# A three-stage kernel on one core: the low parts of expert weights, all made by VectorE instead of half by GpSimd

## The chip, the core and the metric

The kernel runs on one core of a Trainium2 chip. The metric is the device time of one execution in microseconds (us). Times before and after are medians of several runs; the profile is one further execution with the hardware profiler on. The engines are named as in the profile's rows: PE (TensorE matmuls), PEld (TensorE weight loads), DVE (VectorE), ACT (ScalarE), POOL (GpSimd) and SP (SyncE, which here only issues DMAs).

## What is computed

Three layers follow one another: a gated linear attention, a dense layer with squared ReLU, and a mixture of experts in which every token goes to one of eight experts. Everything is float32.

```python
def _moe2_ref(x, w_gate, w1, w2):        # x: 3072 x 384, w1: 8 x 384 x 1024, w2: 8 x 1024 x 384
    logits = x @ w_gate
    expert_idx = np.argmax(logits, axis=1)
    ...
    for e in range(E):
        mask = expert_idx == e
        ...
        h = np.maximum(x[mask] @ w1[e], 0.0)
        out[mask] = gate_w[mask, None] * (h @ w2[e])

def reference(**kwargs):
    attn_out = _attn_ref(**attn_kwargs)               # gated linear attention, 4 x 8 heads, 768 x 48
    ...
    x = _moe_ref(x=x, **moe_kwargs)                   # h = relu(x @ w_in); h * h @ w_out, 384 -> 2048 -> 384
    return _moe2_ref(x=x, **moe2_kwargs)
```

## The kernel before, in words

**Products in three parts.** A float32 matrix product is done as three matmuls in the type fp32r. Each operand is split into a high part, its copy rounded to fp32r, and a low part, the operand minus its high part. The product is then low times high, plus high times low, plus high times high. Every expert weight therefore needs a split before PE can use it: ACT copies the raw tile to `w_hi` (L612), and a tensor-tensor subtraction on DVE or POOL makes `w_lo` (L613). Both lines are in `split_part`.

**Stages.** Up to about 480 us, attention groups alternate with the dense layer, whose eight groups of 384 tokens are interleaved with the next group's attention. From about 480 to 545 us the last dense group runs alone; in it, `ph` (L404) is the first product, `gg`, `gh`, `gl` (L410 to L417) its activation and split, `po` (L434) the second product. From about 546 us to the end the experts run.

**Expert steps.** The experts are worked off in 16 steps that are set out in `KINDS`: 12 steps of kind D (256 token slots of one expert) and 4 of kind S (128 slots). A step gathers its tokens by an indirect DMA (`xg`, L620, POOL's queue), and has eight slots `i`. In slot `i`, `step_h` makes one 128-wide part of the hidden layer, `ph` (nine matmuls, L981; in an S step six or so plain float32 matmuls on the raw weights, L969), then `hh` (ACT, L985) and `hl` (DVE, L986). `step_out` multiplies `hh` and `hl` with the second weight matrix into `qo` (D) or `qs` (S, L1001). It runs two slots later in a D step and three later in an S step. At a step's end ACT scales the result (`o`, L1013), and POOL's queue scatters it to `out` (L1014).

**Weights.** An expert's weights are loaded in eight pieces, `rawt[j]` for j = 0 to 7, 384 KB each (L634, SP's queue). In the listings of instructions below these eight buffers are called raw_5241 (j = 0) to raw_5248 (j = 7). Pieces 0 to 3 hold the first matrix, 4 to 7 the second. Piece `j` of step `s` is split into the set `wst_[s % 2][j]`, w_hi_154 for even steps and w_hi_155 for odd ones, each with its own `w_lo`. An S step splits only pieces 4 to 7. `split_plan` fixes in which slot each piece is split. As soon as a piece is split, the next step's load into the same `rawt[j]` is issued on SP's queue, which is worked off in order and holds these loads one behind the other.

**Who sets the order.** PE and ACT run in the order in which the program is written. The order on DVE, POOL and SP in the expert steps comes from a scheduler that simulates the program. Each engine then runs its own list strictly in order.

**The line in question.** `split_w` (called from `run_steps` for steps 1 to 15) gives the subtraction to POOL for the pieces in `lo_pool(s)`: j = 1, 3, 5, 7, or 3, 5, 7 when the step before is of kind S. Step 0's pieces are split in the last dense group by a direct call of `split_part`, always on DVE.

Of the kernel before, what the change touches and what calls it, by code (L numbers as in the profile page):

```python
# [19 lines left out]
B, H, S, D = 4, 8, 768, 48  # L20
# [15 lines left out]
KINDS = "DD" + "DDDSDDSDDSDDDS" + "SSS"  # L36
# [20 lines left out]
def gla_moe_moe_kernel(ctx: ExitStack, tc: tile.TileContext, qk, ft, vt, w_in, w_out, w_gate, w_gateT, w_e, q, k, v, f_logit, out, dbg=None):  # L57
    nc = tc.nc
# [548 lines left out]
    rawt, xg = [], []  # L607
    wst_ = []
    ids_t, esi_t, reg_t, x_s, out_t = {}, {}, {}, {}, {}

    def split_part(hi, lo, src, eng=nc.vector):
        nc.scalar.activation(out=hi, in_=src, func=AF.Copy)  # L612
        eng.tensor_tensor(out=lo, in0=src, in1=hi.bitcast(F32), op=ALU.subtract)  # L613
# [331 lines left out]
    early["split"], early["ready"] = [], False  # L945
    SPLITS = split_plan()


    def lo_pool(s):
        return (3, 5, 7) if KINDS[s - 1] == "S" else (1, 3, 5, 7)  # L950

    def split_w(s, j):
        if s == NEARLY - 1:
            early["split"].append(j)
        split_part(*wst_[s % 2][j], rawt[j], nc.gpsimd if j in lo_pool(s) else nc.vector)

    def wslice(s, which, a, n):
        j, o = divmod(a, WP)
# [85 lines left out]
    def run_steps(s0, s1, hook=None, pend=(), flush=True):  # L1044
        pend = list(pend)
        for s in range(s0, s1):
            if s == NALWAYS - 1:
                tc.mark_branch_hint_location("rest")
            for i in range(8):
                pend.append((s, i, *step_h(s, i)))  # L1050
                while len(pend) > (2 if KINDS[s] == "D" else 3):
                    step_out(*pend.pop(0))
                if i == 0 and s + 2 != NEARLY:
                    load_x(s + 2)
                if KINDS[s] == "S" and i % 2:
                    load_w(s + 1, i // 2)
                for t, j in SPLITS.get((s, i), ()):
                    split_w(t, j)
                    if t + 1 != NEARLY or early["ready"]:
                        load_w(t + 1, j)  # L1060
                if hook:
                    hook(s, i)
                if i == (5 if KINDS[s] == "D" else 3):
                    prep_next(s + 1)
        if flush:
            for p in pend:
                step_out(*p)
        return pend
# [302 lines left out]
```

## Time and profile before

| | before |
|---|---|
| median of 3 runs | 824.01 us (823.91 to 825.7) |
| the profiled execution | 823.52 us |
| its span, first to last instruction | 821.7 us |
| mean granted TensorE clock | 0.989 of full speed |
| PE busy | 785.1 us, 96% |
| DVE busy | 548.8 us, 67% |
| ACT busy | 414.2 us, 50% |
| POOL busy | 159.9 us, 19% |

The span is what the profile's times count from; about 1.8 us of the execution lie outside it. Busy time is the time in which an engine worked on an instruction, including any time in which that instruction itself was held up. A granted clock of 1.00 is 2.4 GHz, and 0.50 is 1.2 GHz.

### The profile page before, as it was taken

To read this page: it belongs to the slowest core of one execution; us is meant where nothing else is said; L and a number is where in the kernel's file an instruction comes from. 1 tells how busy PE (TensorE), PEld (TensorE's weight loads), DVE (VectorE), ACT (ScalarE), POOL (GpSimd) and SP (SyncE) were. 2 spreads that over 40 slices of the span, in tenths; PEclk is the share of its full clock that TensorE was granted. 3 is DMA by queue.
4 is the path that set the end of the run, shared out by engine and by line. 5 is a ranking of instruction groups with operands and counts; after the bars stand their busy time and mean duration, and the time that the engine had idled before them with its cause. 6 is when DMAs were issued, how large, how long until landed. Compare 5 with 4: busy or idle time off the path is not lost.

```text
span 821.7 us, 15286 instructions
## 1 busy us (share of the span) xinstructions
PE 785.1 (96%) x5681; PEld 729.6 (89%) x5681; DVE 548.8 (67%) x1266; ACT 414.2 (50%) x830; POOL 159.9 (19%) x158
## 2 busy tenths in 40 slices
PE   5799999999999999999999999989999999999995
PEld 4566679999999999999999999989999899898995
DVE  7979779768768767767767654568566545656641
ACT  2233466455455454454455454753465465555651
POOL 2000000000000000000000011212656466555551
PEclk9899999999999999999999999999999999999998
DMA  9886321112131121130120015314666766758640
GB/s 266 238 266 179 126 47 52 45 53 56 43 88 38 49 63 45 46 98 25 45 69 1 2 43 205 107 59 168 238 210 223 255 218 206 268 177 277 203 143 29
DMA packets 40563, 102.09 MB, mean 124 GB/s; under 512 B 5630, under 2 KB 9442, under 8 KB 40352
## 3 DMA queue, kind: packets, MB, share of 16 engines
q1 hardware_dynamic: 36896, 91.57, 36.3%
q0 software_dynamic: 3584, 9.46, 3.1%
q8 instruction: 47, 0.77, 0.4%
q14 instruction: 36, 0.29, 0.1%
HBM read 91.31 MB, written 10.24 MB: 124 GB/s over the span
## 4 chain that ended last, share of the span: by engine, by line
PE 76%; DVE 8%; issue 6%; DMA 5%; ACT 4%; POOL 1%; SPq 0%; POOLq 0%; DVEq 0%; ACTq 0%
PE po L434 22%; PE ph L404 20%; PE qo L1001 8%; PE ph L981 8%; DVE w_lo L613 4%; PE ph L394 4%; DMA raw<-w_e 3%; PE pa L263 3%; PE py L319 3%; ACT w_hi L612 2%; PE ph L969 1%; PE py L299 1%; PE pu L309 1%; PE qs L1001 1%; DMA xT<-xT 1%
## 5 line engine op out<-in xcount | busy, mean ns | idle before, releaser
L410 ACT ACTIVATE gg<-ph 128x384 f32<-128x384 f32 x128 | 62.7, 490 | 180.8 <-PE ph L404 128.3
L417 DVE TENSOR_TENSOR gl<-gg,gh 128x384 fp32r<-128x384 f32 x112 | 63.4, 566 | 84.4 <-ACT gh L415 83.2
L404 PE MATMUL ph<-xh,w_lo 128*128 128x384 f32 x336 | 118.7, 353 | 0.9 <-ACT gg L410 0.9
L434 PE MATMUL po<-w_hi,gl 128*128 128x384 f32 x336 | 113.8, 339 | 2.2 <-DVE gl L417 2.2
L404 PE MATMUL ph<-xl,w_hi 128*128 128x384 f32 x336 | 114.4, 340 | 0.6 <-DVE xl L162 0.6
L404 PE MATMUL ph<-xh,w_hi 128*128 128x384 f32 x336 | 113.9, 339 | 0.0
L434 PE MATMUL po<-w_hi,gh 128*128 128x384 f32 x336 | 113.7, 338 | 0.0
L434 PE MATMUL po<-w_lo,gh 128*128 128x384 f32 x336 | 113.2, 337 | 0.0
L613 DVE TENSOR_TENSOR w_lo<-raw,w_hi 128x768 fp32r<-128x768 f32 x63 | 94.4, 1500 | 24.0 <-ACT w_hi L612 18.2
L613 POOL TENSOR_TENSOR w_lo<-raw,w_hi 128x768 fp32r<-128x768 f32 x49 | 91.1, 1875 | 82.8 <-ACT w_hi L612 80.4
L612 ACT ACTIVATE w_hi<-raw 128x768 fp32r<-128x768 f32 x112 | 93.8, 839 | 19.8 <-DMA raw<-w_e 19.6
L986 DVE SCALAR_TENSOR_TENSOR hl<-ph,hh 128x256 fp32r<-128x256 f32 (+1 forms) x128 | 48.8, 387 | 78.8 <-ACT hh L985 76.3
L985 ACT ACTIVATE hh<-ph 128x256 fp32r<-128x256 f32 (+1 forms) x128 | 45.2, 356 | 97.5 <-PE ph L981 72.4
L708 POOL MEMSET xg<- 128x385 f32 x4 | 1.5, 422 | 466.9 <-DVE gl L417 466.9
L981 PE MATMUL ph<-xh,w_lo 128*128 128x256 f32 x288 | 82.8, 288 | 5.9 <-DVE w_lo L613 5.9
L458 DVE SCALAR_TENSOR_TENSOR junk<-rows,wgb 128x384 f32<-128x384 f32 x144 | 80.0, 555 | 3.3
L981 PE MATMUL ph<-xl,w_hi 128*128 128x256 f32 x288 | 81.4, 283 | 0.0
L981 PE MATMUL ph<-xh,w_hi 128*128 128x256 f32 x288 | 81.1, 282 | 0.0
L411 ACT ACTIVATE gg<-gg 128x384 f32<-128x384 f32 x128 | 67.2, 525 | 4.0
L404 PEld LDWEIGHTS ph<-xh,w_lo 128*128 128x128 f32 x336 | 63.0, 187 | 6.9 <-issue 3.1
L1001 PE MATMUL qo<-w_hi,hl 128*128 128x384 f32 x192 | 66.4, 346 | 1.7 <-DVE hl L986 1.3
L434 PEld LDWEIGHTS po<-w_hi,gl 128*128 128x128 f32 x336 | 63.3, 189 | 2.8 <-DVE gl L417 2.5
(236 smaller groups left out, 1653.9 us busy)
## 6 DMA issues: line engine op xcount, KB each, us to landing
raw<-w_e SPq DMA_DIRECT2D x128, 384.0 KB
qk<-qk SPq DMA_DIRECT2D x46, 192.0 KB
v<-vt SPq DMA_DIRECT2D x24, 256.0 KB
stg<-w_in SPq DMA_DIRECT2D x8, 768.0 KB
stg<-w_out SPq DMA_DIRECT2D x8, 768.0 KB
f<-ft SPq DMA_DIRECT2D x24, 226.2 KB
xs<-rows SPq DMA_DIRECT2D x8, 577.5 KB
wgb<-w_gateT SPq DMA_DIRECT2D x1, 1536.0 KB
```

The costliest lines, as they stand in the source:

```text
L404: nc.tensor.matmul(ph, lhsT=w[:, sl], rhs=x[:, k, :], start=(n == 0), stop=(n == 8))
L410: nc.scalar.activation(out=gg, in_=ph, func=AF.Relu)
L411: nc.scalar.activation(out=gg, in_=gg, func=AF.Square)
L417: nc.vector.tensor_tensor(out=gl, in0=gg, in1=gh.bitcast(F32), op=ALU.subtract)
L434: nc.tensor.matmul(po[m], lhsT=a[:, sl], rhs=w[:, ws], start=(i == 0 and n == 0), stop=(i == NF - 1 and n == len(terms) - 1),)
L458: nc.vector.scalar_tensor_tensor(out=junk, in0=rows[:, m, 0:DM], scalar=1.0, in1=wgb[0][:, e, :], op0=ALU.mult, op1=ALU.mult, accum_out=lg ...
L612: nc.scalar.activation(out=hi, in_=src, func=AF.Copy)
L613: eng.tensor_tensor(out=lo, in0=src, in1=hi.bitcast(F32), op=ALU.subtract)
L981: nc.tensor.matmul(ph, lhsT=wslice(s, w, (i * 3 + k) * 128, 128), rhs=x[:, k, :], start=(n == 0), stop=(n == 8))
L985: nc.scalar.activation(out=hh, in_=ph, func=AF.Relu)
L986: nc.vector.scalar_tensor_tensor(out=hl, in0=ph, scalar=0.0, in1=hh.bitcast(F32), op0=ALU.max, op1=ALU.subtract)
L1001: nc.tensor.matmul(out_t[s][m], lhsT=x[:, sl], rhs=wslice(s, w, 3 * F2 + i * DM, DM), start=(i == 0 and n == 0), stop=(i == 7 and n == 2),)
```

## The change

`lo_pool` goes, and `split_w` no longer passes an engine, so every subtraction goes to `split_part`'s default, VectorE:

```diff
-    def lo_pool(s):
-        return (3, 5, 7) if KINDS[s - 1] == "S" else (1, 3, 5, 7)
-
     def split_w(s, j):
         if s == NEARLY - 1:
             early["split"].append(j)
-        split_part(*wst_[s % 2][j], rawt[j], nc.gpsimd if j in lo_pool(s) else nc.vector)
+        split_part(*wst_[s % 2][j], rawt[j])
```

The program on PE and on ACT stays the same instruction for instruction. DVE's list grows by 49 subtractions, which POOL's list loses, and SP keeps its loads in the same order, with some reads of a register value moved between the first loads of step 2. Line numbers behind the edit shift by 4, so L986 is L982 afterwards.

**Where an S step ends and a D step begins.** The listing below is DVE's, from the fifth slot of the first S step (step 5) on. Before:

```order
L613 TENSOR_TENSOR w_lo<-raw_5247,w_hi_154 128x768
L986 SCALAR_TENSOR_TENSOR hl<-ph_7281,hh 128x128
L643 TENSOR_TENSOR xl_7299<-px,xh_7298 128x3x128 x2
L986 SCALAR_TENSOR_TENSOR hl<-ph_7314,hh 128x128
L986 SCALAR_TENSOR_TENSOR hl<-ph_7325,hh 128x128
L613 TENSOR_TENSOR w_lo<-raw_5241,w_hi_154 128x768
L986 SCALAR_TENSOR_TENSOR hl<-ph_7340,hh 128x128
L986 SCALAR_TENSOR_TENSOR hl<-ph_7351,hh 128x128
L613 TENSOR_TENSOR w_lo<-raw_5242,w_hi_154 128x768
```

The same place now:

```order
L613 TENSOR_TENSOR w_lo<-raw_5247,w_hi_154 128x768
L982 SCALAR_TENSOR_TENSOR hl<-ph_7281,hh 128x128
L613 TENSOR_TENSOR w_lo<-raw_5248,w_hi_154 128x768
L643 TENSOR_TENSOR xl_7299<-px,xh_7298 128x3x128 x2
L982 SCALAR_TENSOR_TENSOR hl<-ph_7314,hh 128x128
L982 SCALAR_TENSOR_TENSOR hl<-ph_7325,hh 128x128
L613 TENSOR_TENSOR w_lo<-raw_5241,w_hi_154 128x768
L982 SCALAR_TENSOR_TENSOR hl<-ph_7340,hh 128x128
L982 SCALAR_TENSOR_TENSOR hl<-ph_7351,hh 128x128
L613 TENSOR_TENSOR w_lo<-raw_5242,w_hi_154 128x768
```

Piece 7's subtraction (raw_5248) came from POOL's list. It now stands ahead of the split of the gathered tokens (`xl`) and four rows ahead of piece 0 of the D step (raw_5241).

**Within a D step.** DVE's list in step 2, where the pieces of step 3 are split; `hl` is one row per slot. Before:

```order
L986 SCALAR_TENSOR_TENSOR hl<-ph_6606,hh 128x256
L613 TENSOR_TENSOR w_lo<-raw_5241,w_hi_155 128x768
L986 SCALAR_TENSOR_TENSOR hl<-ph_6640,hh 128x256
L986 SCALAR_TENSOR_TENSOR hl<-ph_6663,hh 128x256
L613 TENSOR_TENSOR w_lo<-raw_5245,w_hi_155 128x768
L986 SCALAR_TENSOR_TENSOR hl<-ph_6686,hh 128x256
L613 TENSOR_TENSOR w_lo<-raw_5243,w_hi_155 128x768
L643 TENSOR_TENSOR xl_6711<-px,xh_6710 128x3x128 x2
L986 SCALAR_TENSOR_TENSOR hl<-ph_6726,hh 128x256
L986 SCALAR_TENSOR_TENSOR hl<-ph_6749,hh 128x256
```

Now:

```order
L982 SCALAR_TENSOR_TENSOR hl<-ph_6606,hh 128x256
L613 TENSOR_TENSOR w_lo<-raw_5241,w_hi_155 128x768
L982 SCALAR_TENSOR_TENSOR hl<-ph_6640,hh 128x256
L613 TENSOR_TENSOR w_lo<-raw_5242,w_hi_155 128x768
L982 SCALAR_TENSOR_TENSOR hl<-ph_6663,hh 128x256
L613 TENSOR_TENSOR w_lo<-raw_5245,w_hi_155 128x768
L982 SCALAR_TENSOR_TENSOR hl<-ph_6686,hh 128x256
L613 TENSOR_TENSOR w_lo<-raw_5243,w_hi_155 128x768
L643 TENSOR_TENSOR xl_6711<-px,xh_6710 128x3x128 x2
L982 SCALAR_TENSOR_TENSOR hl<-ph_6726,hh 128x256
L613 TENSOR_TENSOR w_lo<-raw_5246,w_hi_155 128x768
L982 SCALAR_TENSOR_TENSOR hl<-ph_6749,hh 128x256
```

Slots that had no subtraction between two `hl` now have one; no two stand next to each other here.

**At the end of the last dense group.** DVE's list where pieces of step 0 (w_hi_154) and step 1 (w_hi_155) are split between the `gl` of that group. Before:

```order
L417 TENSOR_TENSOR gl<-gg,gh 128x384 x2
L613 TENSOR_TENSOR w_lo<-raw_5243,w_hi_154 128x768
L417 TENSOR_TENSOR gl<-gg,gh 128x384
L613 TENSOR_TENSOR w_lo<-raw_5244,w_hi_154 128x768
L613 TENSOR_TENSOR w_lo<-raw_5243,w_hi_155 128x768
```

Now:

```order
L417 TENSOR_TENSOR gl<-gg,gh 128x384
L613 TENSOR_TENSOR w_lo<-raw_5242,w_hi_155 128x768
L417 TENSOR_TENSOR gl<-gg,gh 128x384
L613 TENSOR_TENSOR w_lo<-raw_5243,w_hi_154 128x768
L417 TENSOR_TENSOR gl<-gg,gh 128x384
L613 TENSOR_TENSOR w_lo<-raw_5244,w_hi_154 128x768
L613 TENSOR_TENSOR w_lo<-raw_5243,w_hi_155 128x768
```

Piece 1 of step 1 (raw_5242 with w_hi_155) is made by DVE between two `gl`; everything else keeps its order.

## Rows read from the trace of the kernel before

**Rows 1.** Waits of PE, 500 to 822 us: total us, times, longest.

```profile
PE ph L981 <- DVE w_lo L613: 5.9, 3, 2.0
PE po L434 <- DVE gl L417: 2.2, 1, 2.2
PE qo L1001 <- DVE hl L986: 1.3, 7, 0.2
```

**Rows 2.** Groups by line and shape: busy us, mean ns | idle before.

```profile
L613 DVE TENSOR_TENSOR w_lo<-raw,w_hi 128x768 fp32r<-128x768 f32 x63 | 94.4, 1500 | 24.0 <-ACT w_hi L612 18.2 <-issue 5.4 <-DMA raw<-w_e 0.3
...
L613 POOL TENSOR_TENSOR w_lo<-raw,w_hi 128x768 fp32r<-128x768 f32 x49 | 91.1, 1875 | 82.8 <-ACT w_hi L612 80.4 <-DMA raw<-w_e 2.1
L417 DVE TENSOR_TENSOR gl<-gg,gh 128x384 fp32r<-128x384 f32 x112 | 63.4, 566 | 84.4 <-ACT gh L415 83.2
...
L986 DVE SCALAR_TENSOR_TENSOR hl<-ph,hh 128x256 fp32r<-128x256 f32 x96 | 39.9, 421 | 61.7 <-ACT hh L985 60.5 <-issue 0.5
...
L162 DVE TENSOR_TENSOR w_lo<-w_raw,w_hi 128x768 fp32r<-128x768 f32 x16 | 15.3, 956 | 4.4 <-ACT w_hi L161 4.3
```

**Rows 3.** Timeline at the first change from S to D: start, us, engine.

```profile
649.46 1.82 POOL L613 TENSOR_TENSOR w_lo<-raw,w_hi 128x768 fp32r<-128x768 f32 x1
649.48 2.62 DVE L613 TENSOR_TENSOR w_lo<-raw,w_hi 128x768 fp32r<-128x768 f32 x1 [0.45 <-issue]
...
652.15 0.39 PE L981 MATMUL ph<-xh,w_lo 128*128 128x256 f32 x1 [1.97 <-DVE w_lo L613]
652.20 0.85 ACT L612 ACTIVATE w_hi<-raw 128x768 fp32r<-128x768 f32 x1 [1.83 <-DMA raw<-w_e]
```

**Rows 4.** Timeline within a D step.

```profile
592.39 4.79 DVE L613 TENSOR_TENSOR w_lo<-raw,w_hi 128x768 fp32r<-128x768 f32 x1 [0.31 <-ACT w_hi L612]
592.69 3.67 POOL L613 TENSOR_TENSOR w_lo<-raw,w_hi 128x768 fp32r<-128x768 f32 x2
597.11 0.74 DVE L986 SCALAR_TENSOR_TENSOR hl<-ph,hh 128x256 fp32r<-128x256 f32 x2
```

**Rows 5.** Chain of waits, 596 to 605 us: start, us, what.

```profile
597.57 1.32 PE qo L1001 x6
...
600.59 1.06 PE qo L1001 x6
```

**Rows 6.** Chain of waits, 649 to 660 us.

```profile
652.15 1.51 PE ph L981 x9
...
655.59 1.54 PE ph L981 x9
```

**Rows 7.** Chain of waits, 697 to 706 us: the second change from S to D.

```profile
701.35 1.32 PE ph L981 x9
...
703.72 1.07 PE ph L981 x9
...
705.31 0.71 PE ph L981 x6
```

**Rows 8.** Windows: busy us of PE, PEld, DVE, ACT, POOL; PEclk; DMA share; GB/s.

```profile
544.00:546.00 2.00, 2.00 (x8) 2.00 (x7) 1.72 (x4) 0.57 (x2) 0.00 (x0) 0.50 0.31 54
...
654.00:656.00 2.00, 2.00 (x8) 2.00 (x8) 1.47 (x3) 0.82 (x2) 0.00 (x0) 0.50 1.06 349
```

**Rows 9.** Timeline of DVE in the last dense group.

```profile
521.27 1.35 DVE L417 TENSOR_TENSOR gl<-gg,gh 128x384 fp32r<-128x384 f32 x1 [3.09 <-ACT gh L415]
```

**Rows 10.** Timeline at the end of the last dense group.

```profile
540.28 0.85 ACT L612 ACTIVATE w_hi<-raw 128x768 fp32r<-128x768 f32 x1 [2.04 <-DMA raw<-w_e]
...
542.65 0.79 DVE L417 TENSOR_TENSOR gl<-gg,gh 128x384 fp32r<-128x384 f32 x1 [3.34 <-ACT gh L415]
...
543.49 0.44 PE L434 MATMUL po<-w_hi,gl 128*128 128x384 f32 x1 [2.15 <-DVE gl L417]
```

**Rows 11.** Timeline at 666 us: a subtraction beside a DMA issue of POOL.

```profile
666.23 0.96 DVE L613 TENSOR_TENSOR w_lo<-raw,w_hi 128x768 fp32r<-128x768 f32 x1 [0.31 <-ACT w_hi L612]
666.70 1.40 POOL L620 DMA_INDIRECT xg<-xs,ids  x1 [0.67 <-PE px L641]
```

## The prediction

> **What bounds the kernel now.** I read the profile from PE outward. PE is busy 96% of the span, so the first view is what PE waits for in the stretch that the edit touches. From 500 us to the end three waits make nearly all of PE's idle time, and DVE ends each of them [rows 1]: 5.9 us in three pieces until a `w_lo`, 2.2 us in one piece until a `gl`, 1.3 us in seven pieces until an `hl`. The question is then why DVE is late, although it is busy only 67% of the span.
>
> The groups by line answer it. A subtraction of 128x768 on DVE takes 0.956 us in the dense stage, where POOL has nothing of the kind; the same shape at L613, with POOL at work on its own 49, takes 1.50 us on average over 63 [rows 2]. POOL's take 1.875 us each. Then I looked at the places in order of time. At the first change from an S step to a D step, POOL starts a subtraction at 649.46 and ends at 651.28; DVE's, started at 649.48, takes 2.62 us and ends at 652.10, 0.82 us after POOL's; PE, which had run dry 1.97 us before, starts at 652.15 [rows 3]. Within a D step DVE's subtraction of 592.39 lasts 4.79 us, to 597.18, again 0.82 us behind the end of POOL's two back to back at 596.36 [rows 4]. So while POOL runs such an operation, DVE's does not advance, and the reader can see the price of POOL's help: it comes out of DVE's time, and out of the time of what stands behind it in DVE's list.
>
> **The change part by part.** POOL loses 49 operations of 1.875 us. DVE gets 49 of 0.96 us, 47 us of work; it gets back what the overlap cost it, 63 x (1.50 - 0.96) = 34 us, so its busy time should rise by only about 13 us, to some 562 us. What matters is where.
>
> *Changes from S to D, three of them.* Piece 0 of the D step would take 0.96 instead of 2.62 us, end at 650.44, and let PE start at 650.49, 0.31 us after it runs dry: 1.66 us each, 5.0 us for the three waits of 1.97. The added piece 7 now stands four rows ahead of piece 0. DVE was idle for 0.45 us before piece 0 [rows 3] and elsewhere in the S step; if the addition found no other room, piece 0 would start 0.96 - 0.45 = 0.51 us late, 1.5 us over the three. I take nothing for it, since it stands ahead of two `hl` whose inputs come later, and keep 1.5 for the range.
>
> *D steps.* Seven waits for `hl` give 1.3 us [rows 1], 0.19 each. After one, the next six matmuls take 1.32 us instead of 1.06 [rows 5], so a wait costs 0.45 and the seven 3.2 us. An `hl` behind a subtraction of 0.96 us instead of 4.79 comes 3.8 us earlier, and PE waited only 0.19, so the waits go wholly, with over 3 us of slack. The price: other slots now have a subtraction in front of their `hl`. Each can delay its `hl` by at most 0.96 us, under the 3 us, so I cost it at nothing. The cover is the two slots between `hl` and its use; without it each of some 50 slots would cost up to 0.96.
>
> *The clock.* After the first S-to-D wait the clock fell to 0.50 of 2.4 GHz, that is 1.2 GHz [rows 8]. For nine matmuls, six and nine more PE needed 4.98 us, 652.15 to 657.13 [rows 6]; behind the second such wait the same took 3.44 us, 701.35 to 704.79 [rows 7]. With a wait of 0.31 us I expect no fall: 1.5 us. The lower bound is nothing, if the fall has another cause.
>
> *The end of the last dense group.* PE waits 2.15 us for a `gl` that took 0.79 instead of about 0.56 us (the mean of all is 0.566 [rows 2]), because POOL was at work: 0.23 us. That `gl` was late since ACT stood 2.04 us for a load [rows 10], and loads are issued when DVE has done the piece before. A `gl` of 1.35 us at 521.27 [rows 9] held up this chain by 0.79 us. DVE now makes the added piece there itself, just before that `gl`; I keep 0.5 of the 0.79. Together 0.7 us, between 0 and 1.0. Behind this wait too the clock is 0.50 [rows 8]; whether a wait of 1.4 us instead of 2.15 still brings that is open. I leave it as it is; if it goes, another 1.5 us or so goes with it.
>
> *Queues.* SP's loads keep their order, and wait for DVE where they waited for POOL; a piece is done 0.9 us sooner or more, so no load is issued later. The register reads moved between step 2's first loads let its second load start sooner and none later than before; nothing in [rows 1] waits for these loads, so I take nothing for it. POOL's gathers and scatters no longer queue behind subtractions. A DMA issue beside a DVE subtraction takes 1.40 us, and the subtraction stays 0.96 [rows 11]; the issues have POOL almost to themselves now.
>
> Sum: 5.0 + 3.2 + 1.5 + 0.7 = 10.4 us. The profiled execution took 823.52 us, so 813.1; the median of the runs is 0.5 us above it, so **813.6 us**.
>
> A rule that speaks against one term: the Trainium skill, in "SBUF — State Buffer", section "Who interferes with whom", says that DVE operations with two SBUF inputs and GpSimd operations that read SBUF exclude each other, and that whoever issues first holds the ports for the whole instruction. The trace agrees that one blocks the other, but not on the order: DVE's operation began 0.30 us before POOL's and still ended after both [rows 4]. Taken strictly, the rule would not explain the 4.79 us, and the 3.2 us of the D steps would stay; it is the third rival below.
>
> **The rivals.**
>
> *DVE becomes the bound (slower).* One mechanism: subtractions stay long without POOL's, because DMA issues on POOL hold DVE as its subtractions did. A D step lasts 8 x (1.06 + 1.07) = 17.0 us [rows 5, 7], and DVE must then do 8 subtractions and 8 `hl` of 0.42 [rows 2]. At 0.96 that is 11.0 us; it decides at (17.0 / 8) - 0.42 = 1.7 us per subtraction. At POOL's own 1.875 us it is 18.4 us, 1.4 us too much in each of some ten D steps: 14 us more with no wait saved, about 838 us. For it speaks the mean of 1.50; against it the 0.96 us beside a DMA issue [rows 11] and the 0.956 without POOL. Chance 0.03.
>
> The skill's "Perfetto Trace Analysis", section "Optimizing Scalar/DVE Operations", advises to offload when DVE is saturated, and warns that between DVE and GpSimd it might not help, as they share a port. The trace shows 11.0 of 17.0 us, not saturated.
>
> *The wait moves to the load of piece 1.* At the first S-to-D change ACT starts piece 1 at 652.20, having waited 1.83 us for its load [rows 3]; split, it is ready near 654.1. PE needs it with the third group of nine in the D step, 705.31 - 701.35 = 3.96 us after its start [rows 7], so at 654.45 when it starts at 650.49: 0.35 us of slack. Loads that were held behind POOL now start sooner and share the DMA engines. One load of 384 KB at 349 GB/s [rows 8] is 1.1 us; if that much is put in front of piece 1, PE waits 0.75 us, three times: 2.3 us, so 815.9. Against it: piece 1's load is issued before the freed ones. Chance 0.13.
>
> *Only the S-to-D waits shrink*, the `hl` waits having another cause: 816.8. Chance 0.05, as each ends 0.82 us behind POOL in both pictures.
>
> *The clock.* If the fall at 652 us stays in spite of the short wait, 815.1: 0.07. If the one at 544 us goes too, 812.1: 0.22.
>
> *No change* within 0.2% (1.6 us): the waits would have to come back in equal size elsewhere, as for loads: 0.04.
>
> **How the numbers follow.** The forecast has 0.46. Its own case and those of the clock and the load run from 812.1 to 815.9; adding 1.5 for a late piece 0 to the forecast gives 815.1, and up to 0.3 more at the dense group's end and the residual 0.31 three times give 810.9 at the best. With 816.8 included, the range is **811.0 to 817.0**, which leaves out the last case and the slower one, and some of the tails. A measurement of this kernel can tell about 0.2%. Faster by more than that: 0.46 + 0.13 + 0.05 + 0.07 + 0.22 = 0.93, same 0.04, slower 0.03.
>
> **What would show it.** In the profile after, L613 on DVE should be 112 operations of about 0.96 us, and POOL should have none. The three waits of PE for `w_lo` should be about 0.3 us each, those for `hl` gone, the wait for `gl` about 1.4 us, and PEclk 1.00 near 650 us. I am wrong if L613 stays well above 0.96 us, if PE waits in the middle of D steps for `hl`, or if the wait for piece 0 turns into one for piece 1 with a DMA as its releaser.

## The result, and the profile after

The changed kernel took 816.38 us (median of 5 runs, 815.77 to 819.04), the kernel before 825.2 us (5 runs, 823.91 to 827.79) in the same comparison: ratio 0.9897, 95% interval 0.9873 to 0.9922. The gain is 8.8 us where 10.4 were forecast; 816.38 lies inside the range 811.0 to 817.0. The profiled execution took 815.93 us with a span of 814.2, 7.6 us below the 823.52 of before.

Waits of PE from 500 to 822 us in the changed kernel (us in total, times, longest):

```profile
PE po L434 <- DVE gl L417: 1.5, 1, 1.5
PE qo L997 <- ACT o L1009: 1.0, 1, 1.0
PE ph L977 <- DVE w_lo L613: 0.6, 2, 0.4
PE pl L484 <- ACT xt L476: 0.4, 1, 0.4
PE pi L672 <- DVE sel L668: 0.4, 1, 0.4
PE pl L484 <- DVE xt L478: 0.3, 1, 0.3
```

The 5.9 us for `w_lo` of [rows 1] have become 0.6 and the waits for `hl` are gone; those for `o` and `xt` are new, the one for `sel` was there before. Groups by line and shape (busy us, mean ns | idle before):

```profile
L613 DVE TENSOR_TENSOR w_lo<-raw,w_hi 128x768 fp32r<-128x768 f32 x112 | 106.9, 956 | 47.8 <-ACT w_hi L612 44.0 <-issue 2.7 <-DMA raw<-w_e 1.0
L417 DVE TENSOR_TENSOR gl<-gg,gh 128x384 fp32r<-128x384 f32 x112 | 62.0, 554 | 78.4 <-ACT gh L415 74.4 <-ACT gg L411 2.6
```

All 112 subtractions take 0.956 us, against 1.50 in [rows 2]. The first change from S to D, timelines of DVE, ACT and PE:

```profile
648.98 0.96 DVE L613 TENSOR_TENSOR w_lo<-raw,w_hi 128x768 fp32r<-128x768 f32 x1
...
652.84 0.85 ACT L612 ACTIVATE w_hi<-raw 128x768 fp32r<-128x768 f32 x1 [2.25 <-DMA raw<-w_e]
...
654.74 0.39 PE L977 MATMUL ph<-xh,w_lo 128*128 128x256 f32 x1 [0.23 <-DVE w_lo L613]
```

Piece 0 takes 0.96 us instead of 2.62 [rows 3], and PE doesn't wait for it at all. But ACT waits 2.25 us for the load of piece 1, and PE then 0.23 us for that piece. Windows of the changed kernel (columns as in [rows 8]):

```profile
552.00:554.00 2.00, 2.00 (x11) 2.00 (x11) 1.69 (x10) 0.22 (x1) 0.00 (x0) 0.51 0.03 8
...
654.00:656.00 2.00, 1.77 (x13) 1.45 (x13) 2.00 (x4) 1.76 (x4) 0.29 (x1) 1.00 1.01 398
```

The clock stays at 1.00 at 654 us, where it was 0.50. The fall of 544 us has moved to 552 us, behind two new short waits for `xt`. They have a cause on ACT (timeline):

```profile
548.61 0.84 ACT L612 ACTIVATE w_hi<-raw 128x768 fp32r<-128x768 f32 x1 [2.02 <-DMA raw<-w_e]
549.36 0.37 ACT L981 ACTIVATE hh<-ph 128x256 fp32r<-128x256 f32 x1
549.62 0.48 ACT L476 ACTIVATE xt<-pt 128x384 f32<-128x384 f32 x1
```

ACT stands 2.02 us for a load of step 1's piece 6, and `hh` and `xt` queue behind it. In the kernel before it stood 0.69 us there:

```profile
547.63 0.84 ACT L612 ACTIVATE w_hi<-raw 128x768 fp32r<-128x768 f32 x1 [0.69 <-DMA raw<-w_e]
```

**Three stretches.** All kernels of this case have one common mark where the work of the tables ends: the two small products `pi` (L672), each of which waits for `sel` on DVE. The first stands near 491 us, the second where the tables for steps 2 to 15 are done. PE's timeline, before and then after:

```profile
490.67 0.35 PE L672 MATMUL pi<-sel,slot 96*128 96x2 f32 x2 [0.44 <-DVE sel L668]
566.41 0.39 PE L672 MATMUL pi<-sel,slot 96*128 96x18 f32 x2 [0.39 <-DVE sel L668]
```

```profile
492.06 0.35 PE L672 MATMUL pi<-sel,slot 96*128 96x2 f32 x2 [0.43 <-DVE sel L668]
568.19 0.39 PE L672 MATMUL pi<-sel,slot 96*128 96x18 f32 x2 [0.39 <-DVE sel L668]
```

Up to the first mark the change lost 1.39 us, between the marks (566.41 - 490.67 = 75.74, now 76.13) 0.39 us. From the second mark to the end of the span it gained: 821.7 - 566.41 = 255.29 before, 814.2 - 568.19 = 246.01 now, 9.28 us. The experiments are read by these stretches, each from its own profile, beside the medians:

| kernel | median, us (before beside it) | ratio, 95% | first mark | mark to mark | second mark to end |
|---|---|---|---|---|---|
| before | 825.2 | | 490.67 | 75.74 | 255.29 |
| after | 816.38 (825.2) | 0.9873 to 0.9922 | 492.06 | 76.13 | 246.01 |
| before_again | 824.66 (824.37) | 0.9990 to 1.0017 | 490.96 | 76.09 | 255.25 |
| after_again | 816.46 (820.3) | 0.9916 to 0.9961 | 491.88 | 76.47 | 248.05 |
| e1_pool_reads | 820.69 (824.47) | 0.9909 to 0.9955 | 491.58 | 78.89 | 249.13 |
| e2_pool_writes | 824.34 (824.47) | 0.9973 to 1.0005 | 491.06 | 82.51 | 247.23 |
| e3_three_pieces | 820.65 (824.47) | 0.9943 to 0.9969 | 491.57 | 76.04 | 251.29 |
| e4_all_but_three | 818.02 (824.47) | 0.9893 to 0.9935 | 492.06 | 75.38 | 251.26 |
| e5_step1_only | 820.95 (820.3) | 0.9988 to 1.0021 | 491.95 | 76.50 | 251.05 |
| e6_all_but_step1 | 816.45 (820.3) | 0.9938 to 0.9972 | 492.06 | 76.02 | 246.52 |
| e8_pair | 817.09 (824.37) | 0.9888 to 0.9925 | 492.01 | 75.38 | 248.21 |
| e10_act_by_hand | 816.88 (824.37) | 0.9887 to 0.9920 | 491.31 | 77.30 | 246.99 |
| e11_mixed | 815.06 (824.68) | 0.9864 to 0.9904 | 491.99 | 75.35 | 246.66 |

e5, e6, e7 and after_again ran on one chip, on which the kernel before took 820.3 us (817.11 to 823.59, 23 runs) instead of 824 to 825. There the change gained 3.8 us (ratio 0.9916 to 0.9961), less than half of the 8.8.

### The profile page after: what moved, and what is told of

Read it like the earlier page. It is cut to its first block, busy times and chain, and to the rows that moved or that the text cites. A ratio compares the mean times of both kernels' runs of the same rounds, so it can differ in the third digit from the quotient of the medians.

```text
span 814.2 us, 15228 instructions
## 1 busy us (share of the span) xinstructions
PE 782.8 (96%) x5681; PEld 728.7 (89%) x5681; DVE 558.1 (69%) x1315; ACT 413.9 (51%) x830; POOL 78.1 (10%) x109
## 4 chain that ended last, share of the span: by engine, by line
PE 75%; issue 8%; DMA 7%; DVE 4%; ACT 3%; POOL 1%; SPq 0%; POOLq 0%; DVEq 0%; ACTq 0%
PE po L434 22%; PE ph L404 21%; PE qo L997 9%; PE ph L977 8%; DMA raw<-w_e 5%; PE ph L394 4%; PE pa L263 3%; PE py L319 3%; ACT w_hi L612 2%; PE py L299 1%; PE pu L309 1%; DVE w_lo L613 1%; DMA out<-o,ids 1%; DMA xT<-xT 1%; PE pk L256 1%
## 5 line engine op out<-in xcount | busy, mean ns | idle before, releaser
L613 DVE TENSOR_TENSOR w_lo<-raw,w_hi 128x768 fp32r<-128x768 f32 x112 | 106.9, 956 | 47.8 <-ACT w_hi L612 44.0
L404 PE MATMUL ph<-xh,w_lo 128*128 128x384 f32 x336 | 118.6, 353 | 1.4 <-ACT gg L410 1.4
L404 PE MATMUL ph<-xl,w_hi 128*128 128x384 f32 x336 | 114.4, 340 | 0.6 <-DVE xl L162 0.6
L404 PE MATMUL ph<-xh,w_hi 128*128 128x384 f32 x336 | 113.8, 339 | 0.0
L982 DVE SCALAR_TENSOR_TENSOR hl<-ph,hh 128x256 fp32r<-128x256 f32 (+1 forms) x128 | 49.4, 388 | 45.2 <-ACT hh L981 40.9
L404 PEld LDWEIGHTS ph<-xh,w_lo 128*128 128x128 f32 x336 | 63.0, 187 | 7.4 <-issue 3.1
L997 PE MATMUL qo<-w_hi,hh 128*128 128x384 f32 x192 | 65.1, 339 | 0.0
L997 PE MATMUL qo<-w_lo,hh 128*128 128x384 f32 x192 | 65.0, 338 | 0.0
```

The lines of the kernel that those rows point to most:

```text
L404: nc.tensor.matmul(ph, lhsT=w[:, sl], rhs=x[:, k, :], start=(n == 0), stop=(n == 8))
L982: nc.vector.scalar_tensor_tensor(out=hl, in0=ph, scalar=0.0, in1=hh.bitcast(F32), op0=ALU.max, op1=ALU.subtract)
L997: nc.tensor.matmul(out_t[s][m], lhsT=x[:, sl], rhs=wslice(s, w, 3 * F2 + i * DM, DM), start=(i == 0 and n == 0), stop=(i == 7 and n == 2),)
```

## The experiments

**Which half of the change does what.** e3 moves only piece 7 behind an S step; e4 moves all but that.

```diff
 # e3_three_pieces, against before          # e4_all_but_three: (7,) if ... else ()
-        return (3, 5, 7) if KINDS[s - 1] == "S" else (1, 3, 5, 7)
+        return (3, 5) if KINDS[s - 1] == "S" else (1, 3, 5, 7)
```

> The kernel before with only three of the 49 subtractions moved to VectorE: piece 7 of the step after an S step; the other 46 stay on GpSimd. By my sum the terms of the changes from S to D and of the clock at 652 us come, and no other: 5.0 + 1.5 = 6.5 us, less about 0.8 if PE waits for piece 1 there as in the changed kernel: 5.7 to 6.5 us faster, ratio 0.992 to 0.993. Waits for w_lo of piece 0 gone, seven waits for hl still there. Rival (the waits come from all of POOL's work together): under 3 us, ratio above 0.996.

> The changed kernel, but piece 7 of the step after an S step stays on GpSimd (3 subtractions; 46 moved). By my sum only the terms of the D steps and of the dense group's end come: 3.2 + 0.7 us, less the 1.2 to 1.9 us that the changed kernel lost between 545 and 575 us: 2.0 to 2.7 us faster, ratio 0.9967 to 0.9976; the three waits of about 2 us for piece 0 and the clock's fall at 652 us stay. Rival: if the stretch from 545 to 575 us lost its time by chance of the run, 3.9 us, ratio 0.9953.

e3: the seven waits for `hl` stay (1.3 us in all), the clock stays up, and PE's waits for `w_lo` shrink from 5.9 to 2.8 us in four pieces; the last stretch gains 4.0 us. The term of the S-to-D waits with the clock is there, but smaller than the 5.7 us expected, since piece 1 is now waited for. e4: nothing as I expected. Piece 7 is still on POOL, and yet no wait of 2 us is left: `w_lo` 1.5 us in three pieces. POOL and DVE at the first change from S to D in e4:

```profile
650.55 0.96 DVE L613 TENSOR_TENSOR w_lo<-raw,w_hi 128x768 fp32r<-128x768 f32 x1 [0.44 <-ACT w_hi L612]
```

```profile
650.61 1.79 POOL L620 DMA_INDIRECT xg<-xs,ids  x1 [0.31 <-issue]
652.43 1.85 POOL L613 TENSOR_TENSOR w_lo<-raw,w_hi 128x768 fp32r<-128x768 f32 x1
```

DVE's piece 0 began 0.06 us ahead of POOL's second gather. The gather took 1.79 us, and POOL's subtraction came when piece 0 was long done. e4 also has two waits for `hl`, 0.53 us at 664.90 and 0.70 at 757.27, with no operation of POOL near them: there ACT stands 2.5 and 2.7 us for a load, and DVE's subtraction and the `hl` come behind it. e4's six runs lie in two groups, 814.83 to 816.49 and 819.56 to 820.89; the profile is of the second.

**Is that wait a property of the program?** e5 leaves DVE's, POOL's and SP's lists behind the tables word for word as before; e6 is its mirror.

```diff
 # e5_step1_only, against before            # e6_all_but_step1: (1, 3, 5, 7) if s == 1 else ()
-        return (3, 5, 7) if KINDS[s - 1] == "S" else (1, 3, 5, 7)
+        return () if s == 1 else (3, 5, 7) if KINDS[s - 1] == "S" else (1, 3, 5, 7)
```

> The kernel before with only step 1's four subtractions moved (the mirror of the one above; 45 stay). By my sum the dense group's end gives 0.7 us and the stretch to 575 us takes 1 to 2 us back: ratio 1.000 to 1.002. Waits for hl and for the w_lo of piece 0 stay as before. Rival (the prediction's own term alone): 0.7 us faster, 0.999.

> The kernel before once more, unaltered, with a profile. If the three waits of 2 us for the w_lo of piece 0 at the changes from S to D belong to the program, they come again, each behind a subtraction of POOL that began within 0.1 us of DVE's, and the waits after 480 us sum to 18 us as in the first profile. If they hang on the phase in which the scatters and gathers on POOL meet DVE (as the kernels with other subtractions moved suggest, where these waits were 0.7 to 1.2 us), they are shorter here by about a microsecond each, the sum is 13 to 15 us, and the seven waits for hl (0.45 us each) are there in both cases.

before_again has the three waits again, 5.9 us in all, with both subtractions starting at 649.99:

```profile
649.99 2.65 DVE L613 TENSOR_TENSOR w_lo<-raw,w_hi 128x768 fp32r<-128x768 f32 x1 [0.44 <-issue]
649.99 1.82 POOL L613 TENSOR_TENSOR w_lo<-raw,w_hi 128x768 fp32r<-128x768 f32 x1
```

e5 doesn't have them (`w_lo` 2.1 us in three pieces), although nothing there was moved: DVE's piece 0 starts at 650.03, POOL's gather at 650.10 takes 1.79 us, and POOL's subtraction starts at 651.91. In the kernel before, the same gather began at 648.41, 1.07 us ahead of piece 0, and took 1.02 us, which puts the two subtractions side by side. So which of the two comes first is settled by about a microsecond of phase, and the last stretch differs by 4.2 us with it (255.29 against 251.05), as much as e3 gained there by taking POOL's subtraction away. e5's median is no better than that of the kernel before on its chip (820.95 to 820.3); that the kernel before, too, runs in the better phase there would explain both its 820.3 and the smaller gain of after_again, but no profile of it was taken there. What sets the phase is open: ahead of that gather ACT's `hh` waits 1.70 us for PE in the kernel before and 0.57 in e5.

> The changed kernel, but step 1's pieces 1, 3, 5 and 7 stay on GpSimd (4 subtractions; 45 moved). If the loss between 545 and 575 us comes from the four subtractions that moved there, this gets the gain of the later steps and keeps the stretch up to 575 us as in the kernel before: 0.8 us faster than the changed kernel, ratio to before 0.987 to 0.989. Rival: the loss there is chance of phase (which wait a late load meets), not those four: ratio 0.990 or above, and the waits in that stretch sum to 6 us or more again.

> The changed kernel once more, unaltered, beside the three others of this call: ratio 0.988 to 0.992 as in the first measurement. Its profile shows which of the waits between 540 and 580 us come in every execution: if the phase there is fixed by the program, the wait for gl (1.5 us), the two for xt (0.4 and 0.3), and the clock's fall near 552 us come again; if it is chance, they differ by a microsecond or more.

e6 and after_again have the same median (816.45, 816.46). In e6 the wait for `gl` is 2.4 us and none for `xt`, in after_again 1.7 and 0.8; the stretch between the marks is 76.02 and 76.47. My reading of the loss at 545 to 575 us as one of those four subtractions isn't borne out: e4 and e8 have them on DVE too and lose nothing there. What decides is which waits PE meets, each read from PE's timeline (us):

| kernel | step 1's four pieces | wait for `gl` | waits for `xt` | mark to mark | less these waits |
|---|---|---|---|---|---|
| before | POOL | 2.15 | 0 | 75.74 | 73.59 |
| before_again | POOL | 2.63 | 0 | 76.09 | 73.46 |
| e3 | POOL | 2.48 | 0 | 76.04 | 73.56 |
| e6 | POOL | 2.43 | 0 | 76.02 | 73.59 |
| e4 | DVE | 1.82 | 0 | 75.38 | 73.56 |
| e8 | DVE | 1.78 | 0 | 75.38 | 73.60 |
| after | DVE | 1.50 | 0.70 | 76.13 | 73.93 |
| after_again | DVE | 1.73 | 0.79 | 76.47 | 73.95 |
| e5 | DVE | 1.71 | 0.82 | 76.50 | 73.97 |

With the four on DVE the wait for `gl` is shorter in all five kernels, and what PE waits for `gl` and `xt` comes back in full at the second mark. In the six kernels without a wait for `xt` the clock falls to 0.50 (1.2 GHz) behind the wait for `gl`, and ACT stands 0.39 to 1.70 us for the load of piece 6. In the other three the clock stays at 1.00 there, ACT stands 2.02 to 2.14 us for that load, PE waits for `xt`, and the clock falls at 552 us instead; these three take 0.4 us more beyond the waits, which no run takes apart. In after_again the waits for piece 1 are three and 2.1 us, each behind a load; ACT at the third change:

```profile
745.63 0.84 ACT L612 ACTIVATE w_hi<-raw 128x768 fp32r<-128x768 f32 x1 [2.75 <-DMA raw<-w_e]
```

**What makes `hl` late.** e1 and e2 add useless work on POOL to the changed kernel: a subtraction whose result nothing reads, and a memset. e8 puts two real pieces back.

```diff
 # e1_pool_reads, against after, where lo_pool(s) is that of before
+        if j in lo_pool(s):
+            nc.gpsimd.tensor_tensor(out=scr, in0=hi, in1=hi, op=ALU.subtract)   # e2: memset(scr, 0.0), 128x1536
 # e8_pair, against after
+        return () if s == 1 or KINDS[s - 1] == "S" else (1, 7)
```

> The changed kernel, to which 49 subtractions on POOL are added at the places where the kernel before had its own; each subtracts a w_hi from itself into a scratch tile that nothing reads. No weight, load or product waits for POOL's result. My theory (a POOL operation that reads SBUF stops DVE's two-input operation, and this delay is what PE waited for): DVE's L613 rises from 0.96 us to 1.4 us or more in the mean, waits of PE for hl and for the w_lo of piece 0 come back, and 5 to 9 us of the gain of 8.8 are lost: ratio to the kernel before 0.993 to 1.0. Rival (POOL was slow and late by itself, its 1.875 us and its place in the chain of loads held things up): DVE's subtractions may stretch but the time stays near 816 us, ratio 0.990.

> The changed kernel with 49 memsets of a 128x1536 float32 scratch tile on POOL at the same places; they write SBUF and read nothing, and nothing reads the tile. If only reads of POOL stop DVE, L613 stays at 0.96 us and the ratio near 0.990 (816 to 817 us). If any work of POOL on SBUF stops DVE, L613 rises to 1.3 us or more and the ratio goes to 0.993 or above.

> The changed kernel with two pieces of a step that follows a D step put back on GpSimd: 7 and 1, which in the kernel before ran back to back on POOL (piece 7 of one step, then piece 1 of the next) while one subtraction of DVE stood for 4.8 us; step 1 and the steps after an S step have none on GpSimd. My theory (the pair is the whole cause of the waits for hl): these waits of about 0.45 us each in their sum come back at the changes from D to D, some four to seven of them, 1.8 to 3.1 us; L613 on DVE has single operations of 4 us and more; no wait of 2 us for piece 0. So 2 to 3 us slower than the changed kernel, ratio to before 0.3 points above its. Rival (all of POOL's work together makes DVE late): no waits for hl, time of the changed kernel within 1 us.

L613 in e1, and then in e2:

```profile
L613 DVE TENSOR_TENSOR w_lo<-raw,w_hi 128x768 fp32r<-128x768 f32 x112 | 144.9, 1296 | 39.2 <-ACT w_hi L612 34.8 <-PE ph L404 2.4 <-issue 1.4
L958 POOL TENSOR_TENSOR scr<-w_hi 128x768 fp32r<-128x768 f32 x49 | 88.5, 1807 | 67.0 <-ACT w_hi L612 65.5
```

```profile
L613 DVE TENSOR_TENSOR w_lo<-raw,w_hi 128x768 fp32r<-128x768 f32 x112 | 107.0, 956 | 48.3 <-ACT w_hi L612 47.7 <-issue 0.4
L957 POOL MEMSET scr<- 128x1536 f32 x49 | 68.2, 1391 | 42.3 <-PE ph L404 40.3
```

POOL's reads stretch DVE's subtractions (1.296 us), its writes don't (0.956). But in e1 the waits for `hl` and for piece 0 do not come back, and the last stretch loses only 3.1 us against the changed kernel (1.1 against after_again): the theory as I had put it, that any such overlap costs PE time, is wrong. e1's ratio (0.9932) lies in the range that I gave for the theory, but through other waits: where nothing covers the delay, a single read of POOL does cost PE time. DVE, POOL and DVE again at the end of e1's dense group:

```profile
542.87 0.96 DVE L613 TENSOR_TENSOR w_lo<-raw,w_hi 128x768 fp32r<-128x768 f32 x1 [1.93 <-ACT w_hi L612]
...
542.98 2.17 POOL L958 TENSOR_TENSOR scr<-w_hi 128x768 fp32r<-128x768 f32 x1 [3.36 <-ACT w_hi L612]
...
544.35 1.21 DVE L417 TENSOR_TENSOR gl<-gg,gh 128x384 fp32r<-128x384 f32 x1 [0.53 <-ACT gh L415]
```

That `gl` takes 1.21 us instead of 0.56, and PE waits 3.3 us for it, against 1.5. e1's runs are uneven: one took 815.82 us, three 820.58 to 821.30, and the profile is of the slowest. e8 shows what was missing in the D steps. DVE and POOL in e8:

```profile
593.63 4.79 DVE L613 TENSOR_TENSOR w_lo<-raw,w_hi 128x768 fp32r<-128x768 f32 x1 [0.31 <-issue]
...
629.61 3.00 DVE L613 TENSOR_TENSOR w_lo<-raw,w_hi 128x768 fp32r<-128x768 f32 x1 [0.31 <-issue]
```

```profile
593.94 3.65 POOL L613 TENSOR_TENSOR w_lo<-raw,w_hi 128x768 fp32r<-128x768 f32 x2
...
629.91 1.87 POOL L613 TENSOR_TENSOR w_lo<-raw,w_hi 128x768 fp32r<-128x768 f32 x1
```

Beside two POOL subtractions in a row DVE's takes 4.8 us (593.63, 611.63, 766.57), and PE waits for an `hl` when each ends. A fourth wait stands at 578.3, where two of DVE's follow one another, 4.23 us together, with one of POOL's beside them. Beside a single one DVE's takes 3.0 us (629.61, 675.17, 720.34, 784.54), and PE never waits; in e1 the five longest are 2.94 to 2.96 us, with no wait either. So the cover of two slots takes 3.0 us and not 4.2. What made `hl` late was mainly the back-to-back pair of pieces 7 and 1. By the medians e8 can't be told from the changed kernel (0.9907 and 0.9897); the last stretch is 2.2 us longer than in after, 0.2 than in after_again.

Between the marks e1 takes 78.89 us and e2, which loses most there, 82.51. In e2 the memsets wait for nothing but their buffer, run in a row from 543.68 to 565.4 us, and `abr` on DVE goes from 0.35 us (before) to 1.33:

```profile
559.74 1.33 DVE L536 TENSOR_SCALAR abr<-ipos,hf 128x256 fp32r<-128x256 bf16 x1
```

PE waits 4.4 us for `abr`, so e2's median says nothing of the subtractions; its group row does. The Trainium skill, "SBUF — State Buffer", section "Who interferes with whom", says both: two SBUF inputs contend with GpSimd's reads and not its writes, while a tensor_scalar in a two-port mode contends with either. The trace agrees (0.956; 0.35 to 1.33); that `abr` runs in a two-port mode no run shows.

**Can the wait for `gl` be won?** e7 splits step 0's pieces earlier; e10 has ACT follow the program's order in steps 0 and 1, so that step 1's pieces are all split in step 0 (in the kernels before and after, ACT's order in these two steps, too, is the scheduler's, other than said above); e11 splits five of these in the dense group and three at the end of step 0.

```diff
 # e7_earlier, against after
-  {5: [0], 7: [1], 9: [2], 10: [3], 11: [4], 13: [5], 15: [6, 7]}
+  {5: [0], 6: [1], 7: [2], 8: [3], 9: [4], 10: [5], 12: [6], 13: [7]}
 # e10_act_by_hand and e11_mixed, against after
-    with tc.manual_schedule(engines={mybir.EngineType.PE}):
+    with tc.manual_schedule(engines={mybir.EngineType.PE, mybir.EngineType.Activation}):
         left = run_steps(0, NEARLY, hook, flush=False)
 # e11_mixed, in the last dense group's slots, and out of step 0's
+  for j in {6: [0], 8: [1], 10: [2], 11: [3], 12: [4]}.get(i, ()):
+      split_part(*wst_[1][j], rawt[j])
```

> The changed kernel with one more edit: in the last dense group the eight pieces of step 0 are split in slots 5, 6, 7, 8, 9, 10, 12 and 13 instead of 5, 7, 9, 10, 11, 13, 15 and 15, so that the loads of step 1 into the same buffers are issued earlier. My theory (what the changed kernel lost between 545 and 575 us hangs on ACT standing for loads of step 1, which delays gl at 542 us, xt at 549 us and brings the clock down): the wait for gl of 1.5 us shrinks to under 0.5, the two waits for xt go, the clock may stay up at 552 us (1.7 us): 2 to 4 us faster than the changed kernel, ratio to the kernel before 0.985 to 0.987. Rival: more splits per slot delay gh and gl on ACT and DVE in the middle of the group, and PE waits there instead: ratio 0.990 or above.

> The changed kernel, with ACT's order in steps 0 and 1 that of the program instead of the scheduler's, as it is in the later steps. ACT's copies of step 1's pieces then stand in slots 0 to 7 of step 0 instead of between the gg and gh of the last dense group, so ACT no longer stands for step 1's loads at 539, 547 us. My theory: the wait for gl (1.7 to 1.9 us) shrinks to under 0.4, the two waits for xt (1.0 us) go, the clock's fall behind them (1.6 us) goes, and the wait for o near 574 us may change: 3 to 5 us faster than the changed kernel. Rival: step 1's pieces are ready later, or step 2's loads, which follow them, land later, and PE waits for a w_lo at the start of step 1 or 2: no gain or a loss of up to 3 us.

> The changed kernel with ACT's order in steps 0 and 1 that of the program, as in the run before this one, but with step 1's pieces 0 to 4 split in the last dense group (slots 6, 8, 10, 11 and 12, about where the scheduler had put them) and pieces 5, 6 and 7 in slots 5, 6 and 7 of step 0. With all eight in step 0, the table's chain on DVE came late by 3.6 us (waits for abr 1.9 and for sel 1.7) and the clock fell once; with the last three at the end of step 0 nothing of the split stands in front of that chain, and ACT doesn't stand for the loads of pieces 5 and 6 at 539 and 547 us. My theory: waits for gl (1.5), xt (0.7), abr and sel all under 0.5 us, no fall of the clock between 540 and 565 us: 4 to 5 us faster than the changed kernel, ratio to the kernel before 0.984 to 0.986. Rival: step 1 then waits for its last pieces or step 2 for its first (up to 3 us), or the table's chain is the bound without any split in it: ratio 0.988 or above.

e7 took 868.41 us, since from 822 us on it ran extra steps (L1137 to L1150) that the other kernels skip, and so did other work; a write of token rows (L555) had slid behind a load on SP's queue, and whether that brought them is open. Its total can't be compared. Up to there it shows the rival: no wait for `gl`, but 4.0 us in two waits for a `w_lo` inside the dense group (L404). Waits of PE, 500 to 822 us, in e10 and then e11:

```profile
PE pslot L543 <- DVE abr L536: 1.9, 1, 1.9
PE pi L672 <- DVE sel L668: 1.7, 1, 1.7
```

```profile
PE pi L672 <- DVE sel L668: 3.2, 1, 3.2
...
PE po L434 <- DVE gl L417: 0.5, 1, 0.5
```

e10 has no wait for `gl` or `xt`, and PE comes to the same product (`qo`) at 550.43 instead of 555.55 us, 5.1 us earlier; at the second mark nothing is left of it (568.61 against 568.19). In e11 the small waits are down to 0.5 us and the clock stays at 1.00 from 540 to 580 us, and PE then waits 3.2 us for `sel`. The window of e11 before it:

```profile
555.00:560.00 5.00, 5.00 (x39) 4.95 (x38) 5.00 (x29) 1.97 (x5) 0.00 (x0) 1.00 0.00 0
```

DVE is busy all 5.00 us, mostly with the tables. But between them stand the last three pieces of step 1:

```profile
559.54 0.95 DVE L613 TENSOR_TENSOR w_lo<-raw,w_hi 128x768 fp32r<-128x768 f32 x1
...
562.55 0.94 DVE L613 TENSOR_TENSOR w_lo<-raw,w_hi 128x768 fp32r<-128x768 f32 x1
...
564.32 0.96 DVE L613 TENSOR_TENSOR w_lo<-raw,w_hi 128x768 fp32r<-128x768 f32 x1 [0.21 <-ACT w_hi L612]
```

Together they take 2.85 us, and PE waits 3.16 for `sel`; in e10 six subtractions, 5.74 us, stand between the tables. So what PE gained is given back as a wait for the tables' chain on DVE with subtractions in it. The condition of the rival named for e11, no split in that chain, wasn't met, and whether the chain alone would hold up a faster PE is open. The changed kernel has no subtraction among the tables behind `lg` (L485, 552.36), and there DVE itself waits just ahead of `sel`, for ACT's `hh` and so for PE:

```profile
567.21 0.42 DVE L982 SCALAR_TENSOR_TENSOR hl<-ph,hh 128x256 fp32r<-128x256 f32 x1 [0.35 <-ACT hh L981]
...
567.96 0.17 DVE L668 TENSOR_TENSOR sel<-wso,pp 96x18 fp32r<-96x18 f32 x1
```

e11 has the best median (815.06; ratio 0.9864 to 0.9904), but its interval covers that of the changed kernel.

## Why the prediction came out as it did

Faster with 0.93 was right, and the time was 2.8 us above the forecast. From the profiled executions: forecast gain 10.4 us, measured 7.6. By steps:

- *Changes from S to D, 5.0 us.* The three waits went wholly, 5.9 us, and came back as 0.6 us for piece 1. That was the rival with chance 0.13; in after_again it has nearly the price that I gave it (2.1 us against 2.3). That rival's cause, other loads put in front of piece 1, isn't shown: counted from the second mark, ACT takes piece 1 at 652.84 - 568.19 = 84.65 us, before at 652.20 - 566.41 = 85.79. The load isn't later; PE comes earlier still. The cause that my term rests on, POOL's subtraction beside DVE's, is what the trace of before shows twice, but e4 and e5 show that the meeting itself hangs on phase, which I hadn't asked. The added piece 7 ahead of piece 0 cost nothing, as taken.
- *D steps, 3.2 us.* Right: no wait for `hl` is left. The 0.45 us for each was not measured apart. The cause was narrower than "POOL's subtractions": those that held `hl` up for over 4 us. Single ones in the D steps made PE wait for no `hl` (e8, e1). That a subtraction ahead of `hl` costs nothing holds only while its load is in time (e4). And my reading of [rows 4], that the trace disagrees on the order, left out a row: when DVE's subtraction began at 592.39, POOL was at a DMA issue (last section).
- *The clock, 1.5 us.* Right at 652 us. For these three steps, 9.7 us, the last stretch gives 9.28 (after) and 7.2 (after_again).
- *The end of the last dense group, 0.7 us.* This step failed. PE waits 1.5 us for `gl` instead of 2.15, as I had said, and such a gain does reach the second mark; but I took nothing for what PE waits for next. ACT's wait for the load of piece 6 grew from 0.69 to 2.02 us, and PE waits 0.70 us for `xt` behind it. The fall of the clock at 544 us went, as in the rival with chance 0.22, but another came at 552, so that its 1.5 us were not won. The second mark came 0.39 us later, not 0.7 earlier. In e4 and e8, with the same four subtractions on DVE and no wait for `xt`, the stretch is 75.38 us, 0.36 less than before.
- *Not in the sum:* 1.39 us up to the first mark, in a part where no instruction was moved. The other profiles have that mark between 490.63 and 492.06 us: e7, whose edit lies behind it as well, has the 490.63, e4 and e6 the 492.06. So single executions spread that far; but both profiles of the kernel before are low (490.67, 490.96) and both of the changed one high (492.06, 491.88), so whether the edit has a share is open. With it, 1.39 + 1.09 + 0.42 = 2.9 us, the 2.8 that were missing but for rounding.

That the total came so near is partly luck. The largest terms, the waits of 2 us and the clock behind them, rest on a phase of the kernel before: in e5's phase they are mostly gone with nothing moved, and on its chip the same change gained 3.8 us, not 8.8.

DVE didn't become the bound of the D steps: 558.1 us busy, 562 forecast, with 956 ns per subtraction. It holds PE up at the second mark in e10 and e11, where subtractions stand among the tables.

## What to carry to other kernels

An operation that is stretched by a neighbour costs time only past its cover: here 3.00 us were free and 4.79 were not, so look at the longest one and what lies back to back beside it, not at the mean. Before a wait is booked as a gain, follow the path on and ask what the engine waits for next: here a load that had been in time was late once PE came earlier. Where two operations meet by a tenth of a microsecond, give the gain a second value for the other order. The next piece's load is the first candidate for the next wait.

## What the hardware showed

POOL's indirect DMA issues are held up by DVE's subtractions: 1.02 us at 648.41 in the kernel before, with no subtraction beside it, 1.79 at 650.10 in e5 and at 650.61 in e4, where one began 0.07 and 0.06 us earlier; DVE's stays at 0.96. The other way round nothing is seen: in the changed kernel a subtraction begins at 576.71 inside an issue of 575.34 to 577.06 and takes 0.96 us. So between these two POOL pays. "SBUF — State Buffer" of the Trainium skill, in "Who interferes with whom", reports that `tensor_tensor` did not stall such an issue; here it did, and the measurement decides.

Between two subtractions the same section has the order of issue decide who blocks. e1 agrees where POOL had been idle: DVE's began 0.11 us ahead (542.87, rows above), kept its 0.96 us, and POOL's took 2.17 instead of 1.46 to 1.51; the same at 663.54 and 709.85. In e8, as in [rows 4], DVE's began at 593.63, 0.31 us ahead of POOL's, and still took 4.79; there POOL went straight from a DMA issue into its subtraction. The issues, in the kernel before and in e8:

```profile
591.68 1.00 POOL L1014 DMA_INDIRECT out<-o,ids  x1 [0.30 <-ACT hh L985]
```

```profile
592.92 1.00 POOL L1013 DMA_INDIRECT out<-o,ids  x1 [0.30 <-ACT hh L984]
```

Whether that is what turns the order is open: in e1 at 608.25 DVE's began 0.11 us ahead and kept its 0.96, though POOL had come out of a DMA issue 0.04 us before.
